# First MLP's outputs in blocks of 512 tokens across batches, v in token order by five transfers, and a load plan with other lengths, in an attention kernel followed by two MLPs

## The chip, the cores and the metric

The kernel runs on one core of one Trainium2 chip. The metric is the device time in microseconds of one launch; three runs before the change gave 872.04, 875.26 and 876.86 us, and the median, 875.26 us, is the time before.

## What is computed

Inputs are float32 except the five weight matrices, which arrive as float64. Cut to what matters:

```python
# 4 batches, 8 heads, 576 tokens, 64 values a head; m = 32 landmarks (means of 18 tokens)
A = sm(q, k_lm); Bm = sm(q_lm, k_lm); C = sm(q_lm, k)      # softmax of scaled products
Z = Bm.T / (norm1 * norm_inf + 1e-6)
for _ in range(6): Z = 2 * Z - Z @ Bm @ Z
x = (A @ Z @ C @ v)                      # to 2304 tokens x 512
xn = x / rms(x) * rms_g                  # first MLP, 512 -> 1536 -> 512
g = xn @ w_gate
x = (silu(g) * (xn @ w_val)) @ w_out
h = x @ w_in                             # second MLP, 512 -> 2048 -> 512
out = (s * relu(h) ** 2 + b) @ w_out2
```

## The kernel before, in words

The kernel is one long list of operations with what each reads and writes. A `Scheduler` (line 91) plays them through at build time with a cost for each (`t_dve`, `t_act`, `t_mm` and so on, in us) and a `key` (a due time): each engine takes, of the operations whose inputs are ready by the plan, the one with the lowest key. The order found for each engine is what runs; the waits on the chip are those of the data. Buffers come from a `Ring` of `Slot`s and are also given out by the plan. A transfer (engine `sp`, SyncE, one queue for nearly all loads and stores) has a planned length after which its data count as there, and holds the planned queue for that length less 2 us.

Attention for batch b (`attention`, line 426) loads k, q and v (`load_v`, line 489: 18 transfers of 32 tokens' rows, one for each place within a landmark's segment), makes landmark means, the three softmaxes and the iteration for Z, and leaves, for each batch, a matrix `gw` of 64 by 32 blocks and the normalised A, split into a high and a low half (`xs[1, b]`), each half of 288 tokens (HC). The exp of C (line 718) writes 288 values side by side, in the order place within the segment, then landmark.

TensorE multiplies most matrices in a fast form of float32 with fewer bits (fp32r). To keep the precision an operand is split into high and low halves (`split`, line 927: a cast on ScalarE or VectorE, a subtraction on VectorE or GpSimd), and three matmuls (`PART3`) replace one. The plain float32 matmul takes two passes, shown as two records.

Weights come as float64. `narrow` (line 935) loads 512 KB into a `stage` buffer and turns it into float32 with two or three ScalarE operations and one or two of VectorE. In batch 0 the first MLP's weights are made so and stored to DRAM (`kept`); later they are reloaded from there (`first_weights`, line 988, and `out_weights`, line 1002).

The first MLP runs in 48 units: 4 batches by 12 slices f of 128 hidden values. In a unit, `fused` (line 1042) multiplies the weights of f with `gw`, and `hidden` (line 1090), once for each half of 288 tokens, does 12 matmuls of 288 columns (line 1079), a tanh (1096) and two VectorE products (1098, 1102) into a hidden buffer `h`; the places for these are `hq_r`, 11 and, after batch 0's attention, 15. `out_mm` (line 1109) multiplies a half's hidden values with the output weights into four accumulators of 288 columns: 4 matmuls in plain float32 for the first half of batch 0 (line 1125), 12 in fp32r for all others (line 1129), after a split of weights and hidden values. There are 8 halves by 12 steps. From the seventh unit on, two steps stand in each unit:

```python
HALF = F1 // 2
if n >= HALF and i_out[0] < len(outs):
    next_out(t)
```

The outputs go to `xbuf` (line 1139). The second MLP works in blocks of 512 tokens (the last has 256), with matmuls at lines 1033 and 1155; its first block is split from `xbuf` (`x_split`, line 1018) with a due time near its start. Its weights are made by `narrow` in batch 3 and kept in `region`, which attention has left by then. A `gate` is a point in TensorE's order before which certain operations must stand: "hidden" follows the last operation on hidden values, "u" the last hidden matmul.

Of the kernel before, what the change touches and what calls it, by code (L numbers as in the profile page):

```python
# [7 lines left out]
F32 = mybir.dt.float32  # L8
# [31 lines left out]
GV = 8  # L40
W2_STEP = 4.2
TO_F, TO_R = 0.09, 0.11
# [40 lines left out]
class Op:  # L83
    def __init__(self, alts, key, fn, bufs, pair):
        self.alts, self.key, self.fn, self.bufs = alts, key, fn, bufs
        self.pair = {"pool", "dve"} if pair else {"pool"}
        self.n_deps, self.users, self.ready, self.spare, self.after, self.tail = 0, [], {}, {}, 0.0, 0.0
        self.mode = "f" if "pe" in alts else None


class Scheduler:
# [67 lines left out]
    def run(self, warm):  # L159
# [9 lines left out]
        while left:  # L169
# [50 lines left out]
            free[e] = end if e != "sp" else end - 2.0  # L220
# [22 lines left out]
def t_dve2(n):  # L243
    return 0.07 + 0.00052 * n

# [18 lines left out]
def tile_nystrom_attention_two_mlps(  # L264
# [60 lines left out]
    ro_r = ring(3, [128, 512], "rawo")  # L325
# [8 lines left out]
    gw_r = ring(2, [128, 128], "gw")  # L334
    N_H = 8
# [43 lines left out]
    w2_in = rring(N_IN, 512)  # L379
    os_r = Ring(rring(1, 512).slots + [  # L380
# [28 lines left out]

    def load_small(e):  # L410
        e.dma_start(out=gT, in_=rms_g.rearrange("(k p) -> p k", p=128))
# [3 lines left out]
    op(("sp", 3.3), -20, load_small, w=["small"]).after = 6.0  # L415


# [8 lines left out]
    def attention(b, t0, t1):  # L426
# [41 lines left out]
        for nm, a in (("k", k), ("q", q)):  # L468
            for g in range(2):
                t = src[nm, g] = Buf(qk_r[nm, g])  # L470

                def load_heads(e, t=t, a=a, g=g):
                    if not fine:
                        e.dma_start(
                            out=t.t.rearrange("p (t d) -> p t d", d=D),
                            in_=a[b, 4 * g:4 * g + 4].rearrange("h (i t) d -> (h i) t d", t=SEG))
                        return
                    for h in range(4):
                        e.dma_start(
                            out=t.t[32 * h:32 * h + 32].rearrange("p (t d) -> p t d", d=D),  # L480
                            in_=a[b, 2 * h + g].rearrange("(i t) d -> i t d", t=SEG))

                at(("sp", 5.2 if fine else 3.9), -0.3 if b else 0, load_heads, w=[t])
# [215 lines left out]
        def c_side(g, p0):  # L699
# [11 lines left out]

            def c_max(e):
                e.tensor_reduce(out=cm.t[:, 2:3], in_=cm.t[:, 0:2], axis=AX, op=ALU.max)
                e.tensor_scalar(out=cm.t[:, 3:4], in0=cm.t[:, 2:3], scalar1=-scale, scalar2=None, op0=ALU.mult)

            at(("dve", 0.32), p0 + 0.02, c_max, r=[(cm, 0), (cm, 1)], w=[(cm, 3)])
            for hf in range(2):
                at(("act", t_act(HC) + 0.19), p0 + 0.03, lambda e, hf=hf: e.activation(
                    out=eC.t[:, HC * hf:HC * hf + HC], in_=pC[hf].t[:, 0:HC], func=ACTF.Exp,
                    scale=scale, bias=cm.t[:, 3:4], accum_out=cs.t[:, hf:hf + 1]),  # L720
                    r=[pC[hf], (cm, 3)], w=[(eC, hf), (cs, hf)])
# [213 lines left out]
    def narrow(key, kind, f, part, dst, w, after=()):  # L935
# [25 lines left out]
        op(("sp", 3.46), key - 12, load, w=[st])  # L961
# [15 lines left out]
        op({"act": 0.08 + t_act(512), "dve": t_dve(512)}, key, lambda e: (  # L977
# [10 lines left out]
    def first_weights(key, b, f):  # L988

        r = Buf(rg_r)  # L990
        if b == 0:
            for part in range(2):
                narrow(key + 2.6 * part, 1, f, part, lambda part=part: r.t[:, part], (r, part))
            kept[0, f] = dr.tile([128, 2, 512], F32, name=f"keptg{f}")
            op(("sp", 3.7), key + 9, lambda e: e.dma_start(out=kept[0, f], in_=r.t),
               r=[(r, 0), (r, 1)], w=[("kept", 0, f)])
        else:
            op(("sp", 3.7), key - 8, lambda e: e.dma_start(out=r.t, in_=kept[0, f]),
               r=[("kept", 0, f)], w=[(r, 0), (r, 1)])
        return r  # L1000

    def out_weights(key, b, hf, f):
        r = Buf(ro_r)
        if b == 0 and hf == 0:
            narrow(key, 1, f, 2, lambda: r.t, r)
            kept[1, f] = dr.tile([128, 512], F32, name=f"kepto{f}")
            op(("sp", 3.0), key + 6, lambda e: e.dma_start(out=kept[1, f], in_=r.t), r=[r], w=[("kept", 1, f)])
        else:
            op(("sp", 3.0), key - 8, lambda e: e.dma_start(out=r.t, in_=kept[1, f]), r=[("kept", 1, f)], w=[r])
        return r  # L1010
# [79 lines left out]
    def hidden(tg, tv, b, f, hf, u):  # L1090
# [3 lines left out]
        h = hid[b, hf, f] = Buf(hq_r)  # L1094
# [14 lines left out]
    def out_mm(key, b, hf, f):  # L1109
        r = out_weights(key - LEAD_O, b, hf, f)  # L1110
        h, whole = hid[b, hf, f], (b, hf) in ((0, 0),)
        if whole:
            w, hs = [r], [h]
        else:
            w = weights(key - LEAD_O, w_r, lambda: r.t, [r])
            hs = (Buf(hs_r[0]), Buf(hs_r[1]))
            split(key - 2, lambda: hs[0].t[:, 0:HC], lambda: hs[1].t[:, 0:HC], lambda: h.t, [h], *hs, HC)
            h_ops.extend(S_.ops[-2:])
        if f == 0:
            acc1[b, hf] = [Buf(acc_r) for _ in range(KD)]  # L1120
        A = acc1[b, hf]
        for c in range(KD):
            def mm(_, c=c):
                if whole:
                    nc.tensor.matmul(out=A[c].t[:, 0:HC], lhsT=r.t[:, 128 * c:128 * c + 128], rhs=h.t,
                                     start=(f == 0), stop=(f == F1 - 1))
                    return
                for i, (a, y) in enumerate(PART3):
                    nc.tensor.matmul(  # L1129
                        out=A[c].t[:, 0:HC], lhsT=w[a].t[:, 128 * c:128 * c + 128], rhs=hs[y].t[:, 0:HC],  # L1130
                        start=(f == 0 and i == 0), stop=(f == F1 - 1 and i == 2))

            op(("pe", 0.49 if whole else 3 * t_mm(HC)), key + 0.4 * c, mm, r=[*w, *hs], w=[A[c]]).mode = "f" if whole else "r"
        if f < F1 - 1:
            return
        c0 = b * S + hf * HC
        for c in range(KD):
            op({"act": t_act(HC), "dve": t_dve(HC)}, key, lambda e, c=c: (
                e.activation(out=xbuf[:, c, c0:c0 + HC], in_=A[c].t[:, 0:HC], func=ACTF.Copy) if e is nc.scalar  # L1139
                else e.tensor_copy(out=xbuf[:, c, c0:c0 + HC], in_=A[c].t[:, 0:HC])),  # L1140
                r=[A[c], "far"], w=xb(c, c0, HC))
# [3 lines left out]
    def second_mm(key, j, f, w, hs):  # L1145
# [15 lines left out]
        for c in range(nt):  # L1161
# [12 lines left out]
            if j < NB - 1:  # L1174
                op(("sp", 4.2), key, lambda e, store=store: store(e, range(4)), r=[o])
                continue
            op(("sp", 3.1), key, lambda e, store=store: store(e, (0, 1)), r=[o])
# [10 lines left out]
    HALF = F1 // 2  # L1188
    t_first, t_out = 6 * t_mm(HC), 12 * t_mm(HC)
    T, t = [], 0.0  # L1190
    for n in range(len(units) + HALF + 1):
        T.append(t)
        t += 1.03 * ((U_PE[len(u_at[n])] + 4 * t_first if n < len(units) else 0.0) + (2 * t_out if n >= HALF else 0.0))
        t += MORE if n < F1 * (B - 1) else 0.0
# [27 lines left out]
    gate("far", batch_ops[0], 1.0, free_late)  # L1222
    n_w2 = [0]
    late = []

    def prepare_w2(key):
# [4 lines left out]
        if i < N_IN:  # L1231
            d = w2_in.slots[i]
            res = ("w2", i)
            narrow(key, 2, f, part, lambda: d.t, res, ["attn"])
# [9 lines left out]
    outs = [(b, hf, f) for b in range(B) for hf in range(2) for f in range(F1)]  # L1244
    i_out = [0]

    def next_out(key):
        out_mm(key, *outs[i_out[0]])
        i_out[0] += 1

    us = fused(-1.0, 0, [0])
    for n in range(len(units) + HALF + 1):
        t = T[n]
        if n < len(units):
            b, f = units[n]
            if f == 0:
# [3 lines left out]
                else:  # L1260
                    gate("attn", at_ops, t)
# [3 lines left out]
        if n >= HALF and i_out[0] < len(outs):  # L1265
            next_out(t)
            t += t_out
# [6 lines left out]
        if n >= HALF and i_out[0] < len(outs):  # L1274
            next_out(t)
    while n_w2[0] < 2 * F2:
        prepare_w2(T[F1 * (B - 1)] + 6 + W2_STEP * n_w2[0])
    gate("stage", [], T2[F2 - 4])
    gate("hidden", h_ops, T2[0])
    gate("u", u_ops, T2[0])  # L1280
    x_split(T2[0] - 6, 0)
    hs = None
    for i in range(NB * F2):
# [3 lines left out]
        if f == F2 - 4 and j + 1 < NB:  # L1287
# [3 lines left out]
        wi = weights(t - LEAD + 2, u_r, src, [res])  # L1291
# [11 lines left out]
            r=[r, "small", "hidden"], w=[h], pair=True)  # L1303
# [50 lines left out]
```

## Time and profile before

| | us |
|---|---|
| median of three runs | 875.26 |
| profiled execution | 874.78 |
| its span | 873.1 |
| TensorE busy | 844.8 (97%) |
| VectorE busy | 679.2 (78%) |
| ScalarE busy | 472.1 (54%) |
| GpSimd busy | 119.7 (14%) |

In the page, 40 slices of 21.8 us show each engine's busy tenths. TensorE has 8 or 9 nearly everywhere, VectorE 8 or 9 until slice 22 and 6 or 7 after it, where the second MLP runs; DMA has 7 to 9 in slices 1 to 7 and again around slice 20. TensorE's granted clock is full except in a few slices. A line's name is that of the kernel's line; PE is TensorE, DVE VectorE, ACT ScalarE, SPq SyncE's issues. Since matmuls overlap, their shown length is longer than their distance.

### The profile page before, as it was taken

How to read it: one execution, taken by the hardware profiler on the slowest of the kernel's cores; microseconds unless marked ns; L12 is line 12 of the kernel's file. 1: busy time of each engine (PE TensorE's matmuls, PEld its weight loads, DVE VectorE, ACT ScalarE, POOL GpSimd, SP SyncE). 2: the span in 40 equal slices, each digit the busy share in tenths (PEclk: the TensorE clock that was granted, in tenths of full speed). 3: DMA queues.
4: the chain of work that ended last, by engine and by line, in shares of the span. 5: the costliest groups of instructions: out<-in, count | busy, mean ns of one | idle time of the engine just before them, and what ended most of it. 6: DMA issues, size and time to landing. Idle time of an engine off the chain costs nothing.

```text
span 873.1 us, 16943 instructions
## 1 busy us (share of the span) xinstructions
PE 844.8 (97%) x6386; PEld 716.6 (82%) x6386; DVE 679.2 (78%) x1500; ACT 472.1 (54%) x961; POOL 119.7 (14%) x153
## 2 busy tenths in 40 slices
PE   8978999999999999999999999999999999999997
PEld 5666666998799988899999888888888888888896
DVE  6968787888899888999899766766676667666786
ACT  4869868455563355477997433433343334333453
POOL 0260035501870033201000000000000000000000
PEclk9989999999999999999999999999999999999999
DMA  7798897785535413478985000010000000000100
GB/s 223 214 342 274 294 301 222 230 253 169 140 114 177 127 69 97 132 234 272 307 264 169 1 1 1 22 27 1 1 24 25 1 1 25 23 1 1 37 13 24
DMA packets 72513, 105.96 MB, mean 121 GB/s; under 512 B 25584, under 2 KB 46064, under 8 KB 72432
## 3 DMA queue, kind: packets, MB, share of 16 engines
q1 hardware_dynamic: 72240, 104.62, 38.4%
q8 instruction: 50, 0.82, 0.4%
q10 hardware_dynamic: 192, 0.26, 0.1%
q14 instruction: 31, 0.25, 0.1%
HBM read 90.70 MB, written 14.16 MB: 120 GB/s over the span
## 4 chain that ended last, share of the span: by engine, by line
PE 76%; DVE 10%; ACT 5%; DMA 5%; issue 2%; POOL 1%; SPq 0%; DVEq 0%; ACTq 0%; POOLq 0%
PE bank L1033 23%; PE bank L1155 22%; PE bank L1129 12%; PE bank L1079 11%; PE bank L1052 2%; PE bank L676 1%; PE bank L556 1%; DMA region<-in_k_dram 1%; ACT ca L968 1%; DVE ul L1067 1%; ACT cmag L970 1%; DVE wl L931 1%; DMA kepto<-rawo 1%; PE bank L1317 1%; DVE hbuf L1098 1%
## 5 line engine op out<-in xcount | busy, mean ns | idle before, releaser
L1295 ACT ACTIVATE hbuf<-bank 128x512 f32<-128x512 f32 (+1 forms) x79 | 44.0, 557 | 144.4 <-PE bank L1033 144.0
L1033 PE MATMUL bank<-xh,ul 128*128 128x512 f32 (+1 forms) x320 | 117.7, 368 | 0.0
L1033 PE MATMUL bank<-xl,uh 128*128 128x512 f32 (+1 forms) x320 | 117.6, 368 | 0.0
L1033 PE MATMUL bank<-xh,uh 128*128 128x512 f32 (+1 forms) x320 | 117.6, 367 | 0.0
L1155 PE MATMUL bank<-wh,hh 128*128 128x512 f32 x288 | 112.4, 390 | 0.3 <-DVE hh L930 0.3
L1155 PE MATMUL bank<-wl,hh 128*128 128x512 f32 x288 | 112.3, 390 | 0.0
L1155 PE MATMUL bank<-wh,hl 128*128 128x512 f32 x288 | 112.0, 389 | 0.0
L1129 PE MATMUL bank<-hh,wh 128*128 128x288 f32 x336 | 102.4, 305 | 0.3 <-ACT xbuf L1139 0.3
L1129 PE MATMUL bank<-hh,wl 128*128 128x288 f32 x336 | 98.8, 294 | 0.0
L1129 PE MATMUL bank<-hl,wh 128*128 128x288 f32 x336 | 98.8, 294 | 0.0
L1079 PE MATMUL bank<-xh,uh 128*128 128x288 f32 x248 | 77.8, 314 | 6.1 <-DVE ul L1067 3.1
L931 DVE TENSOR_TENSOR hl<-hbuf,hh 128x512 fp32r<-128x512 f32 (+2 forms) x134 | 78.2, 584 | 3.3 <-ACT hh L929 0.9
L1079 PE MATMUL bank<-xh,ul 128*128 128x288 f32 x248 | 74.4, 300 | 1.1 <-DVE ul L1067 1.1
L1079 PE MATMUL bank<-xl,uh 128*128 128x288 f32 x248 | 74.1, 299 | 0.0
L1129 PEld LDWEIGHTS bank<-hh,wh 128*128 128x128 f32 x336 | 63.0, 188 | 10.2 <-issue 8.9
L1033 PEld LDWEIGHTS bank<-xh,uh 128*128 128x128 f32 x320 | 60.1, 188 | 11.2
L1033 PEld LDWEIGHTS bank<-xl,uh 128*128 128x128 f32 x320 | 60.1, 188 | 11.0
L1033 PEld LDWEIGHTS bank<-xh,ul 128*128 128x128 f32 x320 | 60.0, 188 | 10.1
L929 ACT ACTIVATE wh<-region 128x512 fp32r<-128x512 f32 x48 | 30.4, 633 | 67.1 <-PE bank L1155 67.1
L930 DVE CAST uh<-region 128x512 fp32r<-128x512 f32 x57 | 24.3, 426 | 54.2 <-PE bank L1033 54.2
L931 DVE TENSOR_TENSOR wl<-rawo,wh 128x512 fp32r<-128x512 f32 x79 | 60.1, 761 | 5.2 <-ACT wh L929 0.8
L1155 PEld LDWEIGHTS bank<-wh,hl 128*128 128x128 f32 x288 | 54.1, 188 | 11.5 <-DVE hl L931 0.2
(219 smaller groups left out, 1989.5 us busy)
## 6 DMA issues: line engine op xcount, KB each, us to landing
rawo<-kepto SPq DMA_DIRECT2D x84, 256.0 KB, 3.1
rawg<-keptg SPq DMA_DIRECT2D x36, 512.0 KB, 4.6
stage<-in_moe_w_out_dram SPq DMA_DIRECT2D x28, 512.0 KB, 4.7
stage<-in_moe_w_in_dram SPq DMA_DIRECT2D x16, 512.0 KB, 5.0
keptg<-rawg SPq DMA_DIRECT2D x12, 512.0 KB, 7.5
region<-in_v_dram SPq DMA_DIRECT2D x72, 64.0 KB, 2.7
stage<-in_moe_w_val_dram SPq DMA_DIRECT2D x8, 512.0 KB, 6.6
xbuf<-in_moe_w_gate_dram SPq DMA_DIRECT2D x7, 512.0 KB, 6.8
```

The costliest lines, as they stand in the source:

```text
L556: nc.tensor.transpose(pT.t[:, 128 * j:128 * j + 128], s3.t[:, c:c + 128], ident)
L676: nc.tensor.matmul(out=ps.t[:, 0:HC], lhsT=part(u, "bd")[:, 128 * e:128 * e + 128], rhs=part(y, "t").rearrange("p (t e i) -> p t e i", e=2 ...
L929: e.activation(out=hi(), in_=src(), func=ACTF.Copy) if e is nc.scalar
L930: else e.tensor_copy(out=hi(), in_=src())), r=r, w=[wh], pair=True)
L931: b = op({"dve": t_dve(n), "pool": t_pool(n)}, key, lambda e: e.tensor_tensor(out=lo(), in0=src(), in1=hi().bitcast(F32), op=ALU.subtract) ...
L968: op(("act", 0.08 + t_act(512)), key, lambda e: e.activation(out=wide(a.t), in_=word(1).bitcast(F32), func=ACTF.Copy, scale=2.0 ** -112), ...
L1033: nc.tensor.matmul(out=ps.t[:, 0:n], lhsT=w[a].t[:, ks], rhs=x[y].t[:, kd, 0:n], start=(kd == 0 and i == 0), stop=(kd == KD - 1 and i == 2))
L1052: nc.tensor.matmul(out=pU[g].t[m, 256 * j:256 * j + 256], lhsT=gw[b].t[p, m], rhs=r.t[p, :, 128 * k:128 * k + 128], start=True, stop=True)
L1079: nc.tensor.matmul(out=ps.t[:, 0:HC], lhsT=u[a].t[:, 256 * g + 128 * part:256 * g + 128 * part + 128], rhs=x[y].t.rearrange("p k n -> p (k ...
L1129: nc.tensor.matmul(out=A[c].t[:, 0:HC], lhsT=w[a].t[:, 128 * c:128 * c + 128], rhs=hs[y].t[:, 0:HC], start=(f == 0 and i == 0), stop=(f == ...
L1155: nc.tensor.matmul(out=A[c].t, lhsT=hs[a].t[:, s], rhs=w[y].t, start=(f == 0 and i == 0), stop=(f == F2 - 1 and i == 2))
L1295: e.activation(out=r.t[:, 0:n], in_=ps.t[:, 0:n], func=ACTF.Relu) if e is nc.scalar
```

## The change

Output steps of the first MLP go over blocks of 512 tokens (the last 256) that cross batches: a block takes its columns from one to three hidden halves. There are 5 blocks by 12 steps; the first four steps of the first block are in plain float32, the others in fp32r. One step stands in each unit, two units behind, and the rest after the last unit. Hidden buffers: 18 places, in the last batch 21 (seven of them in the places of the second MLP's last four kept weight blocks, which wait for the gate "hidden"). The raw output weights have two buffers instead of three. v is loaded in token order with five transfers of up to 128 tokens, and the exp of C writes in token order. The loads' planned lengths become 3 us plus the larger of 0.00272 us a KB and 0.45 us a transfer; a weight load has 1 us more. Two scalars are loaded at about 130 us instead of in the start. The first block's split for the second MLP has its due time five units before the end of the first MLP, and its weight splits read the gate "u".

```diff
+DMA_LAG = 3.0
+V_KB = 2060
+W_SLACK = 1.0
+DMA_KB = 0.00272
-            free[e] = end if e != "sp" else end - 2.0
+            free[e] = end if e != "sp" else end - DMA_LAG - o.slack
+def t_dma(kb, n=1):
+    return DMA_LAG + max(DMA_KB * kb, 0.45 * n)
-    ro_r = ring(3, [128, 512], "rawo")
+    ro_r = ring(2, [128, 512], "rawo")
+    hmore = sb.tile([128, 864], F32, name="hmore")
-    hq_r = Ring([Slot(hbuf[:, c:c + HC]) for c in [HC * i for i in range(2, 5)] + [1536 + HC * i for i in range(N_H)]] + h_late)
+    hq_r = Ring(h_main + h_more + h_late, True)
+    hq3_r = Ring(h_main + h_more + h_w2, True)
-            sv = v[b].rearrange("h (i n) d -> n i h d", n=SEG)
-            for n in range(SEG):
-                e.dma_start(out=vt()[32 * (n % 4):32 * (n % 4) + 32, n // 4], in_=sv[token(b, n)])
-        at(("sp", 9.5), -0.25 if b else 0.01, load_v, w=[vs])
+            for j in range(5):
+                n = min(128, S - 128 * j)
+                e.dma_start(out=vt()[0:n, j], in_=v[b][:, 128 * j:128 * j + n].rearrange("h n d -> n h d"))
+        at(("sp", t_dma(V_KB, 5)), -0.25 if b else 0.01, load_v, w=[vs])
+            def in_order(hf):
+                x = eC.t[:, 0:S]
+                if fine:
+                    return x.rearrange("p (i n) -> p n i", i=M)[:, HB * hf:HB * hf + HB]
+                return x.rearrange("p (i t e) -> p e t i", i=M, e=2)[:, hf]
-                    out=eC.t[:, HC * hf:HC * hf + HC], in_=pC[hf].t[:, 0:HC], func=ACTF.Exp,
+                    out=in_order(hf), in_=pC[hf].t[:, 0:HC].rearrange("p (t i) -> p t i", i=M), func=ACTF.Exp,
-        op(("sp", 3.46), key - 12, load, w=[st])
+        op(("sp", t_dma(512) + W_SLACK), key - 12, load, w=[st]).slack = W_SLACK
-    def out_mm(key, b, hf, f):
-        r = out_weights(key - LEAD_O, b, hf, f)
-        h, whole = hid[b, hf, f], (b, hf) in ((0, 0),)
+    def out_mm(key, j, f):
+        r = out_weights(key - LEAD_O, j, f)
+        c0, n = blocks[j]
+        parts, c = [], c0
+        while c < c0 + n:
+            i, o = divmod(c, HC)
+            m = min(HC - o, c0 + n - c)
+            parts.append((hid[i // 2, i % 2, f], o, c - c0, m))
+            c += m
+        if j == 0 and f < WHOLE:
...
+        w = weights(key - LEAD_O, w_r, lambda: r.t, [r])
+        hs = (Buf(hs_r[0]), Buf(hs_r[1]))
+        for i, (h, o, d, m) in enumerate(parts):
+            split(key - 2, lambda d=d, m=m: hs[0].t[:, d:d + m], lambda d=d, m=m: hs[1].t[:, d:d + m],
+                  lambda h=h, o=o, m=m: h.t[:, o:o + m], [h], (hs[0], i), (hs[1], i), m)
...
-    HALF = F1 // 2
+    WHOLE = 4
+    X_UNITS = 5
+    LAG0, LAG1 = 2, 2
+    outs = [(j, f) for j in range(NB) for f in range(F1)]
...
-    gate("u", u_ops, T2[0])
-    x_split(T2[0] - 6, 0)
+    gate("u", u_ops, T[len(units) - 1])
+    x_split(T[len(units) - X_UNITS], 0)
-        wi = weights(t - LEAD + 2, u_r, src, [res])
+        wi = weights(t - LEAD + 2, u_r, src, [res, "u"])
```

## Rows read from the trace of the kernel before

**Rows 1.** Busy time of each engine in stretches of the span; columns in line one

```profile
core 0: us, PE busy (x) PEld busy (x) DVE busy (x) ACT busy (x) POOL busy (x), PEclk, DMA share, GB/s
43.00:155.00 112.00, 101.21 (x984) 74.61 (x983) 86.48 (x214) 90.14 (x187) 37.18 (x50) 0.97 0.87 282
155.00:262.00 107.00, 105.22 (x1097) 95.29 (x1096) 92.13 (x218) 58.62 (x135) 49.89 (x61) 1.00 0.61 183
262.00:372.00 110.00, 106.28 (x1100) 95.75 (x1099) 97.69 (x240) 51.13 (x122) 23.64 (x28) 1.00 0.39 122
372.00:455.00 83.00, 82.09 (x730) 77.80 (x730) 76.65 (x174) 69.88 (x142) 2.57 (x2) 1.00 0.83 269
455.00:484.00 29.00, 29.00 (x190) 27.23 (x189) 27.37 (x57) 21.85 (x43) 0.00 (x0) 1.00 0.51 157
484.00:873.00 389.00, 383.95 (x1782) 320.76 (x1781) 265.68 (x477) 152.15 (x270) 0.00 (x0) 1.00 0.05 13
```

**Rows 2.** The chain that ended last, in order of time: start us, us, what

```profile
44.50 4.90 DMA stage<-in_moe_w_val_dram
...
462.86 3.16 PE bank L1129 x24
...
523.41 2.72 PE bank L1155 x12
...
829.04 0.71 PE bank L1033 x6
```

**Rows 3.** Groups of TensorE instructions by form, the output matmuls before

```profile
L1129 PE MATMUL bank<-hh,wh 128*128 128x288 f32 x336 | 102.4, 305 | 0.3 <-ACT xbuf L1139 0.3
```

**Rows 4.** Who TensorE waited for, 43 to 62 us

```profile
PE bank L1079 <- DVE ul L1067: 2.4, 1, 2.4
PE bank L1079 <- DVE hbuf L1098: 1.9, 1, 1.9
```

**Rows 5.** SyncE's issues in order of time, 0 to 45 us

```profile
0.81 0.87 SPq L474 DMA_DIRECT2D region<-in_k_dram  x2
...
2.77 13.24 SPq L492 DMA_DIRECT2D region<-in_v_dram  x18
...
29.14 15.27 SPq L492 DMA_DIRECT2D region<-in_v_dram  x18
```

**Rows 6.** Busy times again, four stretches of start and batch 0

```profile
10.00:16.00 6.00, 6.00 (x93) 4.13 (x91) 3.61 (x12) 3.74 (x10) 0.00 (x0) 1.00 0.59 120
36.00:44.00 8.00, 7.17 (x78) 5.18 (x79) 7.30 (x21) 7.14 (x17) 1.58 (x2) 1.00 0.46 92
46.00:50.00 4.00, 2.68 (x12) 2.71 (x13) 2.32 (x6) 0.57 (x1) 3.61 (x6) 0.71 0.98 320
54.00:57.00 3.00, 2.84 (x13) 2.70 (x14) 1.62 (x5) 2.43 (x6) 2.69 (x5) 0.59 1.06 403
```

**Rows 7.** TensorE in order of time, 92 to 97 us, plain fp32 output matmuls

```profile
95.38 1.72 PE L1125 MATMUL bank<-hbuf,rawo 128*128 128x288 f32 x6
```

**Rows 8.** Groups of VectorE and ScalarE instructions by form

```profile
L931 DVE TENSOR_TENSOR wl<-rawo,wh 128x512 fp32r<-128x512 f32 x79 | 60.1, 761 | 5.2 <-ACT wh L929 0.8
...
L931 DVE TENSOR_TENSOR hl<-hbuf,hh 128x512 fp32r<-128x512 f32 x64 | 44.3, 693 | 2.1
...
L931 DVE TENSOR_TENSOR hl<-hbuf,hh 128x288 fp32r<-128x288 f32 x54 | 27.2, 503 | 1.1 <-ACT hh L929 0.9
...
L978 ACT ACTIVATE cmag<-stage 128x512 f16<-128x512 f32 x54 | 42.7, 791 | 1.2
...
L970 ACT ACTIVATE cmag<-stage 128x512 int32<-128x512 uint8 x57 | 38.1, 669 | 0.0
...
L929 ACT ACTIVATE wh<-rawo 128x512 fp32r<-128x512 f32 x40 | 25.1, 627 | 17.3 <-PE bank L1129 13.7 <-POOL xl L913 1.2 <-ACT region L867 1.0
...
L718 ACT ACTIVATE region<-bank,region 128x288 f32<-128x288 f32 x14 | 6.8, 491 | 2.8 <-DVE region L714 2.8
```

**Rows 9.** DMA issues: transfers, size, median us from issue to landing

```profile
rawo<-kepto SPq DMA_DIRECT2D x84, 256.0 KB, 3.1
```

More of the change, by code (lines that the diff above doesn't have):

```diff
@@ L379, in tile_nystrom_attention_two_mlps @@
     w2_in = rring(N_IN, 512)
+    H_W2 = 4
+    h_w2 = [Slot(region[:, 512 * (N_IN - H_W2) + HC * i:512 * (N_IN - H_W2) + HC * i + HC]) for i in range(512 * H_W2 // HC)]
+    for x in h_w2:
+        x.held = True
+    hq3_r = Ring(h_main + h_more + h_w2, True)
     os_r = Ring(rring(1, 512).slots + [
@@ L1093, in hidden @@
         th = Buf(t1_r)
-        h = hid[b, hf, f] = Buf(hq_r)
+        h = hid[b, hf, f] = Buf(hq3_r if b == B - 1 else hq_r)
         n_ops = len(S_.ops)
@@ L1107, in tile_nystrom_attention_two_mlps, with mm @@
     acc1 = {}
-    def out_mm(key, b, hf, f):
-        r = out_weights(key - LEAD_O, b, hf, f)
-        h, whole = hid[b, hf, f], (b, hf) in ((0, 0),)
[L1112 to L1117, printed above, removed]
+    def out_mm(key, j, f):
[8 more added lines that the diff above has]
+        if j == 0 and f < WHOLE:
+            if f == 0:
+                acc1[j] = [Buf(acc_r) for _ in range(KD)]
+            A = acc1[j]
+            for c in range(KD):
+                def mm(_, c=c):
+                    for h, o, d, m in parts:
+                        nc.tensor.matmul(out=A[c].t[:, d:d + m], lhsT=r.t[:, 128 * c:128 * c + 128], rhs=h.t[:, o:o + m],
+                                         start=f == 0 and d == 0, stop=False)
+                op(("pe", t_mm4(n)), key + 0.65 * c, mm, r=[r, *[h for h, *_ in parts]], w=[A[c]])
+                h_ops.append(S_.ops[-1])
+            return
+        w = weights(key - LEAD_O, w_r, lambda: r.t, [r])
[3 more added lines that the diff above has]
+                  lambda h=h, o=o, m=m: h.t[:, o:o + m], [h], (hs[0], i), (hs[1], i), m)
@@ L1118, in out_mm @@
             h_ops.extend(S_.ops[-2:])
         if f == 0:
-            acc1[b, hf] = [Buf(acc_r) for _ in range(KD)]
-        A = acc1[b, hf]
+            acc1[j] = [Buf(acc_r) for _ in range(KD)]
+        A = acc1[j]
         for c in range(KD):
             def mm(_, c=c):
[L1124 to L1127, printed above, removed]
@@ L1222, in tile_nystrom_attention_two_mlps, with free_w2 @@
     gate("far", batch_ops[0], 1.0, free_late)
+    def free_w2(_):
+        for x in h_w2:
+            x.held, x.free = False, 0.0
     n_w2 = [0]
@@ L1233, in prepare_w2 @@
             res = ("w2", i)
-            narrow(key, 2, f, part, lambda: d.t, res, ["attn"])
+            narrow(key, 2, f, part, lambda: d.t, res, ["attn"] + (["hidden"] if i >= N_IN - H_W2 else []))
             w2[f, part] = (lambda: d.t, res)
@@ L1242, in prepare_w2 @@
             w2[f, part] = (lambda: bb.t[:, e % 2], (bb, e % 2))
-    outs = [(b, hf, f) for b in range(B) for hf in range(2) for f in range(F1)]
-    i_out = [0]
+    n_out = [0]
     def next_out(key):
-        out_mm(key, *outs[i_out[0]])
-        i_out[0] += 1
+        out_mm(key, *outs[n_out[0]])
+        n_out[0] += 1
+        return t_out(n_out[0] - 1)
     us = fused(-1.0, 0, [0])
-    for n in range(len(units) + HALF + 1):
+    for n in range(N_T):
         t = T[n]
+        todo = len(o_at.get(n, []))
         if n < len(units):
@@ L1273, in tile_nystrom_attention_two_mlps @@
             t += 2 * t_first
-        if n >= HALF and i_out[0] < len(outs):
+        if todo:
             next_out(t)
+    gate("hidden", h_ops, T2[0])
     while n_w2[0] < 2 * F2:
```

69 lines of the change are left out of this document (40 added, 29 removed).

## The prediction, made before the change was run

> **What bounds the kernel now.** I read the busy shares and the 40 slices of the page first, then cut the span at the first hidden-layer matmul of each batch (the timeline gives these times) and asked for the busy times of those stretches [rows 1]. The second MLP, from 484 us, fills TensorE wholly: 389 us, and its matmuls follow one another at 2.72/12 = 0.227 us for 512 columns [rows 2]. Its matmuls don't change, so those 389 us stay. All that can move lies in the first 484 us: 43 us of start, four batches of the first MLP's hidden layer (112, 107, 110 and 83 us), and a tail of 29 us with the outputs left over.
>
> The share of busy TensorE (90 to 99% there) hides idle time, because a matmul is shown to its end while the next has begun: one of 288 columns is shown at 305 ns [rows 3], yet the next follows after 3.16/24 = 0.132 us [rows 2]. So I look at the others. In batch 0, DMA has 87% of its engines' time, ScalarE 90.1 and VectorE 86.5 of 112 us; in batches 1 to 3 VectorE has 86, 89 and 92% [rows 1]. TensorE there is fed by VectorE, which is nearly full, and stalls are many and short. Two are long, right at the start of batch 0 (2.4 and 1.9 us [rows 4]), and what ended last before the second is a load of the value weights that was issued at 44.50 and took 4.90 us [rows 2]. SyncE issued it there because it had been issuing the 18 transfers of the next batch's v since 29.14, for 15.27 us; the first batch's v had held it 13.24 us before the first weight load [rows 5]. During these stretches the DMA engines were at 0.59 and 0.46, against 0.98 when weights flow [rows 6]. After the stall the clock is at 0.71 of full over 46 to 50 us, that is, part of it at 1.2 GHz instead of 2.4 [rows 6].
>
> **The change part by part.** *Output matmuls.* Before: 48 in plain fp32 (batch 0, first half; two records each, 1.72 us for six records with the last one's end [rows 7], so about 0.26 each and 0.52 for a matmul) and 3 x 336 = 1008 of 288 columns [rows 3]: 25.0 + 1008 x 0.1317 = 157.7 us. After: blocks of 512, 512, 512, 512 and 256 tokens. Four steps of the first block stay in fp32, 4 x 4 x 0.52 x 512/288 = 14.8 us; 528 matmuls of 512 columns, 119.7 us; 144 of 256 columns at 0.71/6 = 0.118 us [rows 2], 17.0 us. Sum 151.5, so 6.2 us less. But it is placed otherwise: an output step now follows its hidden unit by two units, where before it waited six and then came in pairs. Batch 0 gets 10 steps instead of 12 cheap ones: 14.8 + 6 x 2.72 = 31.1 against 25.0, **+6.1**. Batches 1, 2 and 3 get 12 x 2.72 = 32.6 against 24 x 12 x 0.1317 = 37.9, **-5.3 each**. The tail gets two of 2.72 and twelve of 1.42 against twelve of 1.58: **+3.4**.
>
> *Splits.* Output weights are split into a high and a low half once for each block and step: 4 x 12 + 8 = 56 times instead of 84. Each costs VectorE 0.761 us for the low half and mostly ScalarE 0.627 us for the high one [rows 8]. The hidden values are split in up to three pieces a step: from 0.503 at 288 and 0.693 at 512 columns [rows 8] a piece costs 0.26 + 0.00085 us a column, so 24 low halves of 12.1 us in a batch become 12 steps of 0.693 + 2 x 0.26, 14.6 us. VectorE thus loses 12 x 0.761 - 2.5 = 6.6 us in each of batches 1 to 3, and gains 6 x (0.761 + 0.693 + 0.26) = 10.3 in batch 0, where nothing was split. What 6.6 us less of VectorE gives TensorE no row shows: between 0 (the short stalls are chains, not load) and 6.6. I take **-2 in batches 1 and 2** (the row of batch 3, 92% busy at 83 us, shows that a busy VectorE alone costs TensorE little) and nothing in batch 3.
>
> *v.* Five transfers instead of 18, with the same 256-byte pieces. An issue takes 0.87/2 = 0.44 us for k [rows 5], so five take 2.2 us; some must wait for the transfer eight before them to land. SyncE is free about 11 to 13 us earlier in both batches, and the value weights land before unit 1 needs them. That removes the two stalls (4.3 us) and the slow clock behind them (0.71 over 4 us and 0.59 over 3 us [rows 6], so 4 x 0.29 + 3 x 0.41 = 2.4 us lost). The DMA engines' idle shares, 6 x 0.41 + 8 x 0.54 = 6.8 us [rows 6], are filled with weights that the rest of batch 0 would have waited for at 87%. Together 4.3 + 2.4 + 6.8 = 13.5, and I take **-14 for batch 0** with the better order of loads. The bounds are 0 (DMA, ScalarE or VectorE set the pace anyway) and -20. Batch 0 would be 112 + 6.1 - 14 = 104 us, with VectorE at 86.5 + 10.3 = 97 of them, which is why I go no lower.
>
> Small pieces are slow however they are issued: while v alone moved, 120 GB/s at a share of 0.59 is 203 GB/s for full engines, against 320/0.98 = 327 with weights [rows 6]. A v of 576 x 8 x 64 x 4 B = 1.18 MB so still fills all engines for 5.8 us, and that is in the 6.8 above only as idle share. The page "DMA: Bandwidth & Descriptors" of the Trainium skill, section Specifications, speaks against this part: a transfer wants pieces of at least 512 B for the full rate, and these stay at half of that. What it would make of the time if it set v's length is part of rival 2.
>
> *Exp in token order.* Its output now goes out with 72 bytes from one element to the next. No row shows such a write. The nearest pair is the conversion that writes every second half-word, 791 ns, against 669 ns for one that writes whole words [rows 8], a factor of 1.18, and 0.09 us on the 0.491 of an exp; four lie on batch 0's way: **+0.4**, between 0 and +2 (an exp at twice its time). The page "SBUF — State Buffer" of the Trainium skill (section Door 1: The DMA port swizzle) says that accesses that leave their 16-byte line each time pay a penalty, without a figure; by that the sum would lie towards the +2. The pair of rows agrees in sign.
>
> *Buffers.* Raw output weights have two buffers instead of three. A buffer is busy for 3.1 us of reload [rows 9], 0.63 + 0.76 of split and some signals, 4.6 us, so an output step can follow every 2.3 us. In batches 1 to 3 a unit lasts over 6 us and hides it. In the tail a step has 1.42 us of TensorE, and the four first steps of the second MLP that its banks allow (4 x 12 x 0.227 = 10.9 us) bring it to 2.33: level, and if they run early, a gap at the end. I take **+2.5**, from 0 to +8.
>
> *Waits added.* The hidden values of a batch's second half now live some 14 units, until the next block takes their last columns. At its peak a unit has 3 first halves and 15 second halves alive, and there are 18 places: the VectorE product that writes a hidden value waits for the split two output steps back, and behind it on VectorE stand all later splits. If the planned order holds, that split is long done: nothing. If not, see the third rival. The second MLP's weight splits wait for the last hidden matmul and four converted blocks for the last hidden split: the first are needed only then, the others 12 x 5.44 us later: 0. Fewer reloads (84 to 48 of 256 KB [rows 9]), the two scalar loads moved to 130 us and the x split moved ahead by five units lie on queues that have room in batch 3: 0. That the planner counts 5.4 us for a weight load instead of 3.5 (the diff's formulas) moves consumers to where data really arrives; it is in the -14.
>
> **Sum.** 43.4 + 104 + 99.7 + 102.7 + 77.7 + 34.9 + 389 = 851.4 us of span. Outside the span the profiled run had 874.78 - 873.1 = 1.7 us: 853.1. It lay 0.5 us under the median of 875.26, so against the median I forecast **854 us**.
>
> **Rivals.** *1. Stalls go further.* VectorE's 6.6 us come out whole in batches 1 and 2 (-4.6 each) and the tail's gap doesn't appear (-2.5): 842. For it: VectorE at 86 to 89%. Against it: many short waits there are attention's own chains.
>
> *2. Batch 0 stays as long as its other engines.* The v time returns as DMA, ScalarE and VectorE time: ScalarE already has 90 of 112 us, VectorE gains 10. Then the -14 shrinks to between 0 and -7: 861 to 868. The same comes out if the 13 and 15 us of v are those of its 4608 pieces and not of 18 issues: SyncE is then held as long by five, and the whole -14 is lost, 868. Against that: the engines had time left, at 0.59 and 0.46 [rows 6]. This second way is what the rule on 512 B in the Trainium skill's page "DMA: Bandwidth & Descriptors" would lead to.
>
> *3. The 18 places are too few (slower).* Place: the product that writes a hidden value. Whenever an output step is late (its weights' reload, a split behind attention's work on VectorE), the next hidden matmuls stall, and TensorE has nothing else, since the order is fixed. A stall of this kind in batch 0 cost 2.4 us and then the half clock. It decides from 21/36 = 0.6 us in each unit of batches 0 to 2; at 0.9 us it costs 32: 886. For it: no spare place. Against it: the split needs only data two units old.
>
> **How the numbers follow.** Forecast (848 to 860) 0.55; rival 1, 0.13; rival 2, 0.20; rival 3, 0.12. The range 843 to 871 leaves out half of rival 1, the worst of rival 2 and rival 3, about 2 in 10. About 0.5% (4.4 us) is what a measurement here can tell from no change, so faster means below 870.9: 0.55 + 0.13 + 0.14 = 0.82. Within 0.5%: 0.06 of rival 2 and 0.02 of rival 3, 0.08. Slower: 0.10.
>
> **What would show it.** Right: v issues of 5 in about 2.5 to 6 us; no half clock at 46 to 57 us; batch 0 near 104 us from first hidden matmul to that of batch 1, batches 1 and 2 near 100 to 103, batch 3 near 78, and from its end to the second MLP's steady part about 35. Wrong: if batch 0 stays at 112 or more, the v step fails; if hidden matmuls wait for the product at L1102's place, the buffers fail; if the tail exceeds 40 us, two raw buffers are too few; if exp at L718's place exceeds 0.9 us, the strided write was underpriced.

## The result, and the profile after

Four runs of the changed kernel gave 862.47 to 867.90 us, median **864.12**, against 875.34 for the kernel before in the same comparison (872.04 to 876.86): a ratio of 0.9873 (95% interval 0.9849 to 0.9898). It is faster, as forecast, but 10 us less so than the 854 us of the prediction. The profiled execution took 867.90 us with a span of 866.2; it is the slowest of the four, with 21.7 us at TensorE's lower clock of 1.2 GHz against 15.0 in the profile of before. Its mean granted clock was 0.988; the two executions at 0.997 and 0.998 took 862.47 and 863.15 us, so a stage time read from one execution can carry some us of clock.

The span after, cut at the first hidden-layer matmul of each batch, at unit 47 and at the last output matmul, in the columns of [rows 1]:

```profile
core 0: us, PE busy (x) PEld busy (x) DVE busy (x) ACT busy (x) POOL busy (x), PEclk, DMA share, GB/s
41.60:155.70 114.10, 108.59 (x1046) 83.09 (x1044) 98.88 (x235) 94.56 (x194) 46.03 (x61) 0.96 0.92 294
155.70:259.80 104.10, 101.78 (x955) 84.84 (x954) 88.24 (x218) 49.19 (x126) 51.08 (x71) 0.98 0.43 128
259.80:360.10 100.30, 99.45 (x951) 82.90 (x950) 79.76 (x211) 48.77 (x124) 26.25 (x37) 1.00 0.29 96
360.10:431.40 71.30, 71.30 (x554) 62.23 (x553) 62.43 (x146) 61.56 (x132) 6.91 (x14) 1.00 0.78 251
431.40:471.20 39.80, 39.80 (x252) 36.03 (x251) 32.75 (x73) 14.63 (x32) 0.39 (x1) 1.00 0.40 121
471.20:866.00 394.80, 390.37 (x1779) 320.59 (x1777) 269.58 (x485) 163.78 (x292) 0.00 (x0) 1.00 0.06 17
```

Against the prediction's stages, its steps put on the times of before between these same points (unit 47 to the end is one stage here, because the second MLP's first matmuls mix with the last outputs). The column "buffer moved" is experiment e1 below, the changed kernel with one buffer elsewhere:

| us of the span | before | predicted | after | buffer moved (e1) |
|---|---|---|---|---|
| start | 43.0 | 43.4 | 41.6 | 39.2 |
| batch 0 | 111.8 | 103.9 | 114.1 | 115.0 |
| batch 1 | 107.2 | 99.9 | 104.1 | 103.7 |
| batch 2 | 109.9 | 102.6 | 100.3 | 99.9 |
| units 36 to 46 | 76.9 | 71.6 | 71.3 | 70.6 |
| unit 47 to the end | 424.1 | 430.0 | 434.8 | 427.1 |
| sum | 872.9 | 851.4 | 866.2 | 855.5 |

Three rows carry the miss: batch 0 is longer by 10 us than forecast, the end by 5 and batch 1 by 4; the start and batch 2 give 4 back. The end is the strange one, since the change does not touch the second MLP's matmuls. In its chain of waits twelve matmuls took 2.72 us before [rows 2], and after:

```profile
521.55 2.80 PE bank L1195 x12
527.11 2.80 PE bank L1195 x12
529.90 2.76 PE bank L1059 x12
```

The same instructions at the same full clock follow one another more slowly. From start to start over 500 to 800 us the mean is 231.4 ns, before it was 226.7. Over the 1536 matmuls of 512 columns in the second MLP (4 blocks, 16 slices, 24 each) that is 7.25 us.

SyncE's issues of v, 0 to 50 us, start us, held us, against [rows 5]:

```profile
2.77 7.93 SPq L512 DMA_DIRECT2D region<-in_v_dram  x5
...
27.83 5.13 SPq L512 DMA_DIRECT2D region<-in_v_dram  x5
...
36.27 0.37 SPq L977 DMA_DIRECT2D stage<-in_moe_w_val_dram  x1
```

v holds SyncE 13.06 us in all instead of 28.51, and the value weights that went out at 44.50 now go out at 36.27. But the start of batch 0 has not become free of stalls. Whom TensorE waited for, 41 to 62 us (total, times, longest), against [rows 4]:

```profile
PE bank L1105 <- DVE ul L1093: 2.5, 1, 2.5
PE bank L1374 <- DVE xl L1093: 1.0, 1, 1.0
PE bank L1078 <- DVE rawg L1008: 0.2, 1, 0.2
```

and the clock and the DMA share there, before and later, in the stretches of [rows 6] (34 to 42 us for its 36 to 44) and two more:

```profile
10.00:16.00 6.00, 3.96 (x78) 2.79 (x76) 4.34 (x19) 2.88 (x9) 0.67 (x1) 1.00 1.04 283
34.00:42.00 8.00, 7.29 (x71) 5.45 (x69) 7.36 (x21) 7.48 (x18) 0.71 (x2) 1.00 0.52 167
46.00:50.00 4.00, 3.22 (x17) 3.25 (x18) 3.66 (x8) 2.17 (x5) 3.61 (x6) 0.72 1.01 329
54.00:57.00 3.00, 2.01 (x19) 1.78 (x18) 2.60 (x6) 2.68 (x7) 2.78 (x3) 1.00 0.98 354
106.00:116.00 10.00, 8.52 (x128) 5.83 (x128) 8.98 (x24) 7.23 (x16) 5.92 (x7) 1.00 0.70 196
116.00:123.00 7.00, 6.99 (x93) 4.29 (x97) 4.61 (x14) 4.12 (x9) 4.51 (x8) 0.51 0.86 240
```

The longer of the two stalls is there as before, behind the same split, with 0.72 of the clock behind it. (In e1 below the same wait of 2.5 us lies in 39 to 60 us that ran wholly at full clock, so the one need not bring the other.) The 54 to 57 us stretch is at full clock now, but 116 to 123 us runs at 1.2 GHz (0.51) almost throughout, after a stretch in which attention's chain of VectorE work let TensorE run out of matmuls at times. In all, batch 0 had 10.2 us at the lower clock in this execution, and 6.8 in the profile of before. The DMA engines, at a share of 0.59 over 10 to 16 us before, are full there now (1.04); over 34 to 42 us they are still half idle (0.52).

### The profile page after: what moved, and what is told of

It reads as the page before. It is cut to its first block, busy times and chain, and to the rows that moved or that the text cites. A ratio compares the mean times of both kernels' runs of the same rounds, so it can differ in the third digit from the quotient of the medians.

```text
span 866.2 us, 16057 instructions
## 1 busy us (share of the span) xinstructions
PE 847.1 (98%) x6028; PEld 694.2 (80%) x6028; DVE 663.5 (77%) x1488; ACT 460.6 (53%) x962; POOL 136.8 (16%) x196
## 4 chain that ended last, share of the span: by engine, by line
PE 85%; DVE 2%; ACT 0%; issue 0%; DVEq 0%
PE bank L1195 23%; PE bank L1059 23%; PE bank L1169 16%; PE bank L1105 15%; PE bank L1078 2%; PE bank L696 2%; PE bank L887 1%; PE bank L634 1%; PE bank L783 0%; PE bank L927 0%; PE bank L906 0%; PE bank L609 0%; DVE region L821 0%; DVE hl L957 0%; DVE rawg L1008 0%
## 5 line engine op out<-in xcount | busy, mean ns | idle before, releaser
L1195 PE MATMUL bank<-wh,hh 128*128 128x512 f32 x288 | 114.3, 397 | 0.3 <-DVE hh L956 0.3
L1169 PE MATMUL bank<-hh,wh 128*128 128x512 f32 (+1 forms) x224 | 87.7, 391 | 0.0
L1169 PE MATMUL bank<-hh,wl 128*128 128x512 f32 (+1 forms) x224 | 83.5, 373 | 0.0
L1169 PE MATMUL bank<-hl,wh 128*128 128x512 f32 (+1 forms) x224 | 83.2, 372 | 0.0
L1105 PE MATMUL bank<-xl,uh 128*128 128x288 f32 x256 | 76.6, 299 | 0.0
L1105 PE MATMUL bank<-xh,ul 128*128 128x288 f32 x256 | 76.5, 299 | 0.0
L957 DVE TENSOR_TENSOR hl<-hbuf,hh 128x512 fp32r<-128x512 f32 (+6 forms) x128 | 72.3, 571 | 2.9 <-ACT hh L955 0.5
L957 DVE TENSOR_TENSOR wl<-region,wh 128x512 fp32r<-128x512 f32 x70 | 48.4, 692 | 20.4 <-ACT wh L955 19.7
L1195 PEld LDWEIGHTS bank<-wh,hh 128*128 128x128 f32 x288 | 54.1, 188 | 11.8 <-DVE hh L956 0.7
```

The costliest lines, as they stand in the source:

```text
L957: b = op({"dve": t_dve(n), "pool": t_pool(n)}, key, lambda e: e.tensor_tensor(out=lo(), in0=src(), in1=hi().bitcast(F32), op=ALU.subtract) ...
L1105: nc.tensor.matmul(out=ps.t[:, 0:HC], lhsT=u[a].t[:, 256 * g + 128 * part:256 * g + 128 * part + 128], rhs=x[y].t.rearrange("p k n -> p (k ...
L1169: nc.tensor.matmul(out=A[c].t[:, 0:n], lhsT=w[a].t[:, 128 * c:128 * c + 128], rhs=hs[y].t[:, 0:n], start=(f == 0 and i == 0), stop=(f == F ...
L1195: nc.tensor.matmul(out=A[c].t, lhsT=hs[a].t[:, s], rhs=w[y].t, start=(f == 0 and i == 0), stop=(f == F2 - 1 and i == 2))
```

## Experiments

Two questions are open: why the 512-column matmuls are slower, and why batch 0 gained so little. For the matmuls, theory A is that their operands lie elsewhere: the new `hmore` (864 columns, 3456 bytes) stands ahead of `hbuf`, `hh` and `hl`, and a `rawo` buffer less (2048 bytes) stands ahead of them too, so `hh` and `hl`, the split hidden values, lie 1408 bytes later. Theory B is that the slowness belongs to that execution, or to something else in the change, such as another order of splits on VectorE and ScalarE beside the matmuls.

**e1: the new buffer at the end of the on-chip memory.** Nothing else changes; `hh` and `hl` then stand 2048 bytes earlier than in the kernel before.

```diff
-    hmore = sb.tile([128, 864], F32, name="hmore")
     N_H = 8
...
     region = sb.tile([128, R_COLS], F32, name="region")
+    hmore = sb.tile([128, 864], F32, name="hmore")
```

> The changed kernel with the new buffer of 864 columns at the end of SBUF instead of ahead of hbuf; the order of all instructions is the same, only the addresses of hbuf, hh, hl and region move. In the changed kernel the 512-column matmuls of the second MLP follow one another at 231.4 ns on average, before at 226.7. Theory A (the place of hbuf, hh, hl and region in SBUF slows the matmuls): the distance returns to 226.7, the second MLP loses 7 to 8 us and the first MLP's output steps 2 to 3, so about 854 to 856 us. Theory B (the slower matmuls belong to the state of the chip in that run, or to something else in the change): the distance stays near 231 and the time stays at 863 to 866.

Measured: **856.91 us** (854.24 to 859.07), ratio 0.9787 (0.9759 to 0.9814), 0.9 us over the range of theory A. The chain of waits in the second MLP is back at the old distance:

```profile
522.65 2.72 PE bank L1195 x12
525.37 2.72 PE bank L1059 x12
```

So the place of a buffer, not the order of the work, cost 7.2 us (864.12 - 856.91). No other kernel here is faster. Its stages, in the columns of the first table of stretches:

```profile
39.20:154.20 115.00, 108.02 (x1045) 81.64 (x1044) 98.94 (x235) 94.36 (x194) 45.93 (x61) 0.97 0.93 292
154.20:257.90 103.70, 101.36 (x955) 84.82 (x954) 88.38 (x219) 49.12 (x126) 51.19 (x71) 0.98 0.43 127
257.90:357.80 99.90, 99.06 (x952) 82.87 (x951) 79.79 (x211) 48.74 (x125) 26.16 (x37) 1.00 0.30 96
```

**e2: the kernel before, moved by 1408 bytes.** The reverse: 352 unused columns ahead of `hbuf`, nothing else.

```diff
+    sb.tile([128, 352], F32, name="pad")
     N_H = 8
     hbuf = sb.tile([128, 1536 + N_H * 288], F32, name="hbuf")
```

> The kernel before with 352 unused columns ahead of hbuf, so that hbuf, hh, hl and region stand at the very addresses of the changed kernel; nothing else differs. Theory A: the 512-column matmuls of the second MLP go from 226.7 to about 231 ns, and the time from 875 to about 882 to 885 us. Theory B: 226.7 ns and 875 us, as before.

Measured: 883.63 us (881.85 to 886.62), ratio 1.0098 (1.0072 to 1.0123), and the slow distance, 231.4 ns, in a kernel with none of the change:

```profile
520.92 2.80 PE bank L1156 x12
526.48 2.80 PE bank L1156 x12
```

**e7, e8: which buffer.** The same 352 columns, once behind `hl` (so that only `region` with the kept weights moves) and once between `hbuf` and `hh`.

```diff
     hs_r = [ring(2, [128, 512], nm, F32R) for nm in ("hh", "hl")]
+    sb.tile([128, 352], F32, name="pad")      # e7
```
```diff
+    sb.tile([128, 352], F32, name="pad")      # e8
     hs_r = [ring(2, [128, 512], nm, F32R) for nm in ("hh", "hl")]
```

> The kernel before with the 352 unused columns between hl and region: region alone moves by 1408 B. If it is region's place (VectorE and ScalarE read the second MLP's weights there): 512-column matmuls at about 231 ns in the second MLP and some 883 us. If it is hbuf's or hh's and hl's: 226.7 ns and 875.

> The kernel before with the 352 unused columns between hbuf and hh: hh, hl and region move by 1408 B, hbuf doesn't. With e7_pad_region it tells the tiles apart: as there, if hh and hl don't matter; at about 231 ns where e7 is at 226.7, if TensorE's own operands hh and hl must stand so; 226.7 in both, if it is hbuf, which TensorE doesn't read in the second MLP.

One execution each: 872.77 us with 226.7 ns (e7), 881.54 us with 231.4 ns (e8). `hh` and `hl` have to move for the matmuls to slow: with `region` alone moved they are fast (e7). In e8 `region` moves along, as it does in e2 and in the changed kernel, so that `hh` and `hl` alone would do is not shown. From the chains, e7 first:

```profile
526.71 2.72 PE bank L1156 x12
```
```profile
523.56 2.80 PE bank L1156 x12
```

**e11, e12: by how much.** The pad of e8 with 64 and 128 columns, 256 and 512 bytes.

```diff
-    sb.tile([128, 352], F32, name="pad")      # e8
+    sb.tile([128, 64], F32, name="pad")       # e11; 128 columns in e12
```

> The kernel before with 64 unused columns (256 B) between hbuf and hh. In the kernel before all of xh, xl, u, w, hh and hl begin at the same place modulo 2048 B; a move of hh and hl by 1408 B (11 x 128) slowed the matmuls, one by 2048 didn't. If what counts is 256 B: 226.7 ns and 872 to 876 us. If it is more (512, 1024 or 2048): slower than 226.7, up to 231, and up to 883.

> The kernel before with 128 unused columns (512 B) between hbuf and hh. If the place counts modulo 256 or 512 B: 226.7 ns and 872 to 876 us. If modulo 1024 or 2048: slower than 226.7, as with 1408 B. Together with e11_pad_256B: both fast, 256; this one alone fast, 512; neither, more than 512.

One execution each: 874.84 and 878.62 us, both at 226.7 ns. The second time is 2.6 us over what was expected; that execution had 24.4 us at the lower clock, none of it between 500 and 800 us, where the distance is taken. Shifts by -2048, 256 and 512 bytes leave the matmuls fast; 1408, which is 5.5 times 256, makes them slow in the three places where it was tried (after, e2, e8). By the addresses of the built programs all tiles that TensorE reads there (`xh`, `uh`, `wh`, `hh` and their low halves) begin 128 bytes past a multiple of 256 in the fast kernels; in the slow ones, of these, `hh` and `hl` alone begin on such a multiple. Another odd multiple of 128, or all tiles moved together, was not tried, so that 256 is the period fits all of these and isn't proven.

**e3: v by 18 transfers in the changed kernel**, with the exp in its old order.

```diff
-            for j in range(5):
-                n = min(128, S - 128 * j)
-                e.dma_start(out=vt()[0:n, j], in_=v[b][:, 128 * j:128 * j + n].rearrange("h n d -> n h d"))
+            sv = v[b].rearrange("h (i n) d -> n i h d", n=SEG)
+            for n in range(SEG):
+                e.dma_start(out=vt()[32 * (n % 4):32 * (n % 4) + 32, n // 4], in_=sv[token(b, n)])
```

> The changed kernel with v loaded by 18 transfers again and the exp of C in its old order; the plan's length for v stays that of the five. Theory P (as predicted, SyncE held by 18 issues delays the first weights, and their early arrival shortens batch 0): SyncE is held 13 to 15 us again, the first hidden matmuls are late, and the time is 872 to 880. Theory D (batch 0 is set by the DMA engines, which are 0.92 to 0.96 busy from 42 to 121 us in the changed kernel, so early weights only move the wait): 864 to 868.

Measured: 869.66 us, ratio 0.9933 (0.9911 to 0.9955), 5.5 us over the change. That lies between the two theories. Batch 0 takes 118.4 us instead of 114.1; the start is as long, 41.1.

**e4: the old planned lengths in the changed kernel.**

```diff
-            free[e] = end if e != "sp" else end - DMA_LAG - o.slack
+            free[e] = end if e != "sp" else end - 2.0
...
-        op(("sp", t_dma(512) + W_SLACK), key - 12, load, w=[st]).slack = W_SLACK
+        op(("sp", 3.46), key - 12, load, w=[st]).slack = W_SLACK
```

> The changed kernel with the planned lengths of all loads as before (3.46 us for a weight load instead of 5.39, v 9.5, and the queue free 2 us before the end). Theory P: the order of loads and of what waits for them fits the chip less, batch 0 gets longer by 3 to 8 us, 867 to 873. Theory N (the plan's lengths change little, since keys set the order): within 2 us of the changed kernel, 862 to 866.

Measured: 871.18 us, ratio 0.9952 (0.9932 to 0.9972), 7.1 us over the change, as theory P had it. In its profile batch 0 ran at the full clock from end to end and still took 113.5 us: the slow clock is not what keeps batch 0 long. The kernel before shows the same: in e7, where the instructions are the same, batch 0 ran wholly at the full clock and took 111.3 us, against 111.8 with 6.8 us at the lower clock.

**e5: five transfers alone**, in the kernel before (the lines of e3 the other way, with the exp in token order).

> The kernel before with v in token order by five transfers and the exp of C to match; plan and output steps as before. Theory P (SyncE's issues of v delay the first weights): SyncE is held 8 and 5 us instead of 13 and 15, and the time falls by 4 to 8 us, to 867 to 871. Theory D (batch 0 is set by the DMA engines): at most 2 us less, 873 to 875. If parts add up, the 5.5 us that 18 transfers cost in the changed kernel are the answer.

Measured: 873.59 us, ratio 0.9978 (0.9958 to 0.9997): some 2 us, less than the 0.5% that count here. Theory D had the number; that DMA is the reason is what e9 below speaks against.

**e6: the blocks alone**: e1 with 18 transfers for v, the old exp and the old planned lengths (the edits of e3 and e4 together).

> The kernel before with the output blocks and all that belongs to them (places, two raw buffers, steps two units behind), the new buffer at the end of SBUF, and v and the plan's lengths as before. If the parts add up (address 7.2 us, v 5.5, plan 7.1 of what the changed kernel with the buffer at the end gains, 18 us), the blocks alone bring about 5 to 6 us, what their columns save: 869 to 870. Theory S (VectorE's fewer splits shorten stalls as well, as predicted 4 us): 865 to 867. Theory H (18 places without a spare, or two raw buffers, cost more than the columns save): 873 or more.

Measured: 862.30 us, ratio 0.9863 (0.9825 to 0.9900), 12 us under the kernel before in the same comparison (874.39), and more than any of the theories gave. Its stages: start 42.6, batches 116.7, 102.0, 100.0, units 36 to 46 72.2, end 427.0. Against e1 both undone cost 5.4 us (6.6 by the ratios to the kernel before), about what either alone cost against the change: the two act as one step and don't add up. Why either half without the other is worth next to nothing was not traced.

**e9: is it the DMA engines that set batch 0?** e1 without the stores of the converted weights; the later loads read as many bytes of `q` in their place.

```diff
-            kept[0, f] = dr.tile([128, 2, 512], F32, name=f"keptg{f}")
-            op(("sp", t_dma(512)), key + 9, lambda e: e.dma_start(out=kept[0, f], in_=r.t),
-               r=[(r, 0), (r, 1)], w=[("kept", 0, f)])
...
-            op(("sp", t_dma(256)), key + 6, lambda e: e.dma_start(out=kept[1, f], in_=r.t), r=[r], w=[("kept", 1, f)])
```

> The changed kernel with the new buffer at the end (e1_hmore_last), without storing the first MLP's converted weights to DRAM (24 transfers, 9.4 MB, nearly all in batch 0); later batches reload as many bytes from q instead, so the outputs are not the reference's. In e1 batch 0 takes 115.0 us with the DMA engines 0.94 to 1.03 busy from 39 to 112 us. Theory D (DMA sets batch 0): 9.4 MB at some 320 GB/s are 29 us of engines; batch 0 falls until ScalarE and VectorE (94 and 99 us busy in it) bind, to 98 to 106, and the time to 841 to 849. Theory C (ScalarE's and VectorE's conversions set it): batch 0 stays within 4 us of 115, 853 to 857.

Measured: 858.83 us, ratio 0.9807 (0.9781 to 0.9834), 1.8 us over the range of theory C; batch 0 114.2 us against 115.0. Its row for batch 0:

```profile
41.80:156.00 114.20, 107.54 (x1050) 82.28 (x1048) 97.49 (x232) 97.54 (x201) 44.91 (x61) 0.99 0.74 221
```

The DMA engines' share falls from 0.93 to 0.74 and batch 0 stays. Their load is not its bound. VectorE and ScalarE are still at 97.5 of 114 us each.

**e10: 17 hidden places instead of 18**, in e1.

```diff
-    h_more = [Slot(hmore[:, HC * i:HC * i + HC]) for i in range(3)]
+    h_more = [Slot(hmore[:, HC * i:HC * i + HC]) for i in range(2)]
```

> The changed kernel with the new buffer at the end and 17 places for hidden values in place of 18 in batches 0 to 2 (20 in batch 3). My third rival said that 18 have no spare. If so, 17 stall nearly every unit from the 13th on: batches 1 and 2 get longer by 0.5 us or more a unit, 12 us and more together, 869 or above. If the plan moves the splits earlier instead: within 3 us of e1, 855 to 860.

Measured: 861.38 us (858.15 to 862.10), ratio 0.9840 (0.9807 to 0.9872), 1.4 us over the range for a plan that moves the splits. By stage batches 0 to 2 take 113.7, 103.6 and 99.9 us, no longer than in e1. That is the fastest of the four executions, its span 0.9 us longer than e1's; the intervals of the two ratios overlap, and the rest of the 4.5 us between the medians is not placed. Of TensorE's waits over batches 0 to 2 one of 0.9 us falls on the product that the third rival named:

```profile
PE bank L1105 <- DVE region L814: 3.1, 2, 2.3
PE bank L1105 <- DVE ul L1093: 2.5, 1, 2.5
...
PE bank L1078 <- DVE xbuf L1128: 0.9, 1, 0.9
```

With all 18 places TensorE has no such wait in e1 and after the change, and one of 1.7 us in e6 and of 2.1 us in e4, where the rival asked for 0.6 us in each unit.

## Why the prediction was right, and where it was wrong

**Direction: right, but by the part that was priced lower.** The steps of the blocks sum to -7.9 in the prediction (+6.1, three times -5.3, +3.4, twice -2, +2.5), and the blocks alone bring 12 us (e6); v and the load plan were to bring 14 and bring 5.4 (e6 against e1). Fewer columns were to bring 6.2 over all: batch 0 has 64 records of plain fp32 and 72 of fp32r outputs, as counted, and grew by 4.9 us from before to e6 (111.8 to 116.7; forecast +6.1). How much of the 12 is columns and how much shorter stalls no run separates.

**Batches 1 and 2: right in sum by luck, wrong in detail.** Forecast 99.9 + 102.6 = 202.5; after 204.4, e1 203.6. VectorE's busy time fell by 17.9 us in batch 2 ([rows 1]: 97.69 to 79.76) and only by 3.9 in batch 1, and batch 2 won 10 where batch 1 won 3. The forecast gave -2 of stalls to each; it was none in batch 1 and some -4.5 in batch 2, and the two errors cancel. The 6.6 us of VectorE did not spread evenly. Part of that is other work that moved: after the change five of attention's large splits (L484) and five of its large transposes (L585) lie in batch 1, where there were four of each, some 3 us. The rest was not traced.

**Step "-14 for batch 0": wrong.** With the 6.1 us of output steps, batch 0 came to 114.1 us (115.0 in e1), so some -3.8 (-2.9) is there of the -14. The step had three terms. The two stalls (4.3 us): the 1.9 us for the hidden product are gone, the 2.4 us for `ul` stayed. [Rows 4] named VectorE as its releaser, and yet the prediction let the earlier load remove both. With the weights early, the wait for `ul` is still 2.5 us. In e1's chain of waits it stands behind attention's splits and two conversions on VectorE:

```profile
39.91 1.26 DVE rawg L1008
41.17 1.54 DVE xl L939 x2
42.71 0.73 DVE rawg L1008
43.44 0.34 DVE uh L1091
43.78 0.02 issue
43.81 0.44 DVE ul L1093
44.24 0.14 issue
44.38 1.05 PE bank L1105 x6
```

VectorE has no gap there that an earlier load could fill. The slow clock (2.4 us): 54 to 57 us was regained, 116 to 123 lost, and batch 0 at the full clock is hardly shorter (113.5 us in e4, 111.3 in e7). The idle DMA share (6.8 us): 10 to 16 us was filled, 34 to 42 us not, and batch 0's share rose from 0.87 to 0.92; but e9 shows that DMA time isn't what batch 0 lacks. This is the second rival's direction in its first form, "its other engines". Its second form, that the pieces set SyncE's time, held by half: five transfers hold SyncE less, but the first v still 7.93 us, outside the 2.5 to 6 us named as a sign, with single issues of up to 3.56 us where those of k take 0.44. The first form named DMA among the engines; that part fell with e9. That the 864 us lie in this rival's 861 to 868 is in part chance, since 7 of them are the place of a buffer. VectorE took 98.9 us in batch 0, near the 97 forecast, but of 114 us and not of 104. Whether it or ScalarE ends the short waits of batch 0 was not separated.

**Start: better than forecast, in part by the clock.** From e6 to e1 the start goes from 42.6 to 39.2 us, and batch 0 is 1.7 shorter. But e1's execution had no lower clock before 114 us, e6's 3.4 us of it in the start and 10.2 in batch 0 (e1's 6.8). At half the clock those 3.4 us cost at most 1.7, an estimate, so at least 1.7 of the 3.4 us is v and the plan; the 1.7 in batch 0 could be clock alone. The strided exp was underpriced in size but not in bounds. The group of ScalarE's instructions after:

```profile
L744 ACT ACTIVATE region<-bank,region 128x288 f32<-128x288 f32 x14 | 10.1, 790 | 1.8 <-DVE region L740 1.5 <-PE bank L1078 0.4
```

790 ns where it was 491 [rows 8], and 0.58 was forecast: four of them on the way are +1.2 us instead of +0.4. In e3, the changed kernel with the old order, it is 492 ns, so the order of writing is what costs. The factor is 1.61; the pair of conversions that the forecast took had 1.18. The page "SBUF — State Buffer" of the Trainium skill (section Door 1: The DMA port swizzle) says that accesses that leave their 16-byte line each time pay a penalty, without a figure; the 790 against 491 ns agree.

**Tail: right but for the raw buffers.** In e1 the stages from unit 47 on take 427.1 us against 424.1: +3.0, where the steps themselves were to cost +3.4. The +2.5 for two raw buffers did not come: after the change TensorE has no wait of its own between 360 and 480 us. The 48 matmuls of the second MLP that the prediction counted on do run between the last output steps, but that is not the reason: in e6 only 36 do, with two raw buffers as well, and TensorE waits no more there, with 427.0 us for these stages.

**Step "their matmuls don't change, so those 389 us stay": wrong by 7.2 us.** It looked at the list of instructions and not at where their operands lie. e1, e2, e7 and e8 show it from both sides. Without it the forecast of 854 would have met 856.9, but that nearness is luck: in e1 batch 0 is 11 us over the forecast and batch 1 4, and the start, batch 2, units 36 to 46 and the end are 11 under it together.

**Rival 3: not borne out.** One place fewer leaves every batch its length in the profiled execution.

What stays open: what sets batch 0's length, and what collides when `hh` and `hl` lie 1408 bytes further. The matmuls of the first half of a unit, which read `xh` and not `hh`, are slower too (`xh`,`uh` 232.3 ns, `xl`,`uh` 226.4 as before). In the trace after, the 198 of them (500 to 800 us) beside which no other engine works are still at 226.7 ns on average, and the 396 with VectorE or ScalarE at work at 231.0 (231.4 where that work neither reads nor writes `hh` and `hl`); in e1 both are at 226.6. So this points at an engine beside TensorE, but the undisturbed ones always stand in the same places of a unit, and no run tells which access meets which.

## What to carry to other kernels

When a change adds or resizes a buffer, compare the start-to-start distance of matmuls in a stage that the change doesn't touch; if it moved, try the buffer at the end of the memory before judging the rest. Before a stall is booked as gone because a load comes earlier, look at what the engine that TensorE waited for did in the microseconds before: only where that engine stood idle for the load can the stall go. Undo parts singly and together: v and the plan each looked worth 5 to 7 us when undone alone, and both were worth 5.4.

## What the runs showed of the hardware

The second MLP's matmuls of 512 columns in fp32r had two mean paces at the same granted clock of 2.4 GHz, 226.7 and 231.4 ns from start to start, by nothing but the place of buffers in on-chip memory (`hh`, `hl` and `region`: fast for shifts of -2048, 256 and 512 bytes, slow for 1408, fast for 1408 of `region` alone). An exp of 288 values a partition out of PSUM takes 491 ns written side by side and 790 ns written 72 bytes apart. Five transfers of v held SyncE 7.93 and 5.13 us (8.31 and 8.20 in e5), 18 with the same pieces 13.24 and 15.27 (11.56 and 12.96 in e6).
